# Attention and gated feed-forward on one Trainium2 core: the first unit's attention interleaved over head pairs, and block means placed by a matmul

## The chip, the cores and the metric

The kernel runs on one core of one Trainium2 chip. The metric is the device time of one launch in microseconds (us), the median of several launches. The profile is of one of these launches; its span is 1.7 to 2.1 us shorter than the launch's time. Engines are named as in the profile: PE is TensorE (PEld its weight loads), DVE is VectorE, ACT ScalarE, POOL GpSimd, and SP, which issues DMAs, SyncE. A PE matmul runs at the clock that the throttle grants: full or half (a slow launch also shows 0.95).

## The reference, cut to what matters

The kernel computes attention for 4 batches, 8 heads, 768 tokens, 64 channels, and then a feed-forward layer on all 3072 tokens. A query sees the keys less than 16 positions away, and one summary per block of 32 keys.

```python
k_sum = k.reshape(B, H, nb, block, D).max(axis=3)       # block = 32, nb = 24
v_sum = v.reshape(B, H, nb, block, D).mean(axis=3)
scores_l = scale * q @ k.T, masked to |i - j| < 16
scores_s = scale * q @ k_sum.T + log(block)
a = softmax(concat([scores_l, scores_s]))
x = a @ concat([v, v_sum])                              # per head, then heads side by side
out = x + sigmoid(x @ w_res) * ((gelu(x @ w_gate) * (x @ w_val)) @ w_out)
```

## The kernel before

The work goes in eight units of 384 tokens (half a batch), each with four head pairs. While unit u does its feed-forward, the attention of unit u+1 is woven into its end; at the end of odd units the next batch is prepared too. Only unit 0's attention has nothing to hide behind.

The value tile `vext` holds, for each tile of 64 queries, 96 rows of values (64 plus 16 on each side) and below them 32 rows with the block means, so that one matmul with the masked exponentials P gives both parts and, by a column of ones, the denominator. This product of P with the values is called AV below. The means (`vsum`) are made by a matmul with a constant matrix and then copied, by `vsum_bc`, below every tile. In the code `xn` is the normalised attention output and `xT` its transpose; `sub` counts the three rows of 128 tokens in a unit; MM, AO, TT and SS name PSUM buffers. A column of the feed-forward is 128 of its 1536 hidden channels: four gate and four value matmuls.

```python
def vsum_pair(vs, hp):                     # unit 0: means of one head pair
    for t in range(HT):
        nc.tensor.matmul(vs[96:128, sl], bmat[:, t, :], vext[0][0:BAND, t, ...], start=False, ...)
    nc.vector.tensor_copy(vsum[0][96:128, sl], vs[96:128, sl])
    vsum_bc(0, hp, 0, HT)

def vsum_grp(b, pool, tag):                # other batches: three groups of rows, then moved by DMA
    ...
    nc.vector.tensor_copy(vpart[0:96, :], vs[0:96, :])
    for g, (lo, n) in enumerate(((0, 6), (6, 6), (12, 12))):
        nc.sync.dma_start(out=vsum[b % 2][96 + lo:96 + lo + n, :], in_=vpart[32 * g:32 * g + n, :])

def av_step(u, hp, st, ...):               # 12 matmuls into ao, then the normalisation on DVE
    ...
    nc.vector.reciprocal(rz[:], ao[:, :, :, D:D + 1])
    nc.vector.tensor_mul(xn, ao[:, :, :, 0:D], rz.to_broadcast(...))

# unit 0's attention, after keys, queries and scores
s_step(0, NP - 1, st)
vs = vsum_dense(*TT)
keep_warm(5)                               # matmuls on zeros, result unused
for hp in range(NP):
    vsum_pair(vs, hp)
    av_step(0, hp, st, *(MM if hp % 2 else AO))
    if hp < NP - 1:
        xt_step(0, hp, st, *MM, nc.scalar.copy)      # transpose xn to xT
g0 = half_fo(st, w_gate, 0, 0, KO - 1)               # first feed-forward column
v0 = half_fo(st, w_val, 0, 0, KO - 1)
xt_step(0, NP - 1, st, *TT, nc.scalar.copy)

# end of unit 0: feed-forward of unit 0 and attention of unit 1 (n), woven
s_step(n, 0, nst)
for sub in range(NSUB):
    ffn_step(st, gvT, sub, 0, 4)
    if sub < 2:
        av_step(n, sub, nst); s_step(n, sub + 1, nst)
for sub in range(NSUB):
    ffn_step(st, gvT, sub, 4, 8)
    ...                                              # xt_step 0, av 2, s 3 | xt_step 1, av 3 | xt_step 2
for sub in range(NSUB):
    ffn_step(st, gvT, sub, 8, FO)
    if sub == 1:
        xt_step(n, 3, nst, *TT)
    end_step(u, st, sub)                             # two DVE operations and the store
```

The softmax here doesn't subtract the row's maximum and nothing guards it: scores larger than these inputs give would overflow.

## Time and profile before

The time was 306.99 us (three launches, 305.7 to 307.49). From 115 us to the tail of the last 6 us PE is busy without a gap; what can be won lies before. These are the places:

| place | from, to (us) | PE busy | granted clock |
|---|---|---|---|
| 1, first attention | 16.0, 35.2 | 12.4 of 19.2 | 0.66 |
| 2, end of unit 0 | 54.0, 70.3 | 12.9 of 16.3 | 0.90 |
| 3, end of unit 1 | 91.6, 115.0 | 16.3 of 23.4 | 0.85 |
| the same part of unit 3 | 166.0, 180.0 | 14.0 of 14.0 | 1.00 |

The view of busy time by windows, kernel before. After the window and its length come, for each engine, its busy time and its instructions; then the mean granted clock, the DMA share and GB/s:

```profile
core 0: us, PE busy (x) PEld busy (x) DVE busy (x) ACT busy (x) POOL busy (x), PEclk, DMA share, GB/s
16.00:35.20 19.20, 12.43 (x102) 6.75 (x101) 8.30 (x33) 3.32 (x6) 13.85 (x19) 0.66 1.41 177
53.98:70.30 16.32, 12.93 (x148) 6.58 (x145) 7.84 (x19) 6.95 (x8) 7.96 (x11) 0.90 2.72 152
91.60:115.00 23.40, 16.29 (x159) 7.90 (x159) 11.04 (x24) 7.83 (x9) 6.56 (x9) 0.85 1.35 120
166.00:180.00 14.00, 14.00 (x159) 7.14 (x159) 9.35 (x21) 7.78 (x9) 0.00 (x0) 1.00 0.10 38
```

Place 1. The time line of all engines, kernel before: start, duration, engine, line and operation, output and inputs, number of instructions, and in brackets the idle time before it and what ended it. This is the second head pair:

```profile
22.17 0.81 PE L232 MATMUL vs<-vext,bmat 96*32 96x128 bf16 x6
...
23.02 0.30 DVE L234 CAST vsum<-vs 32x128 bf16<-32x128 f32 x1 [1.18 <-PE vs L232]
23.35 0.36 DVE L256 COPY vext<-vsum 32x768 bf16<-32x768 bf16 x1
23.76 0.54 PE L284 MATMUL ao<-vext,P 128*64 128x65 bf16 x12 [0.78 <-DVE vext L256]
...
24.34 0.20 DVE L288 RECIPROCAL rz<-ao 128x6 f32<-128x6 f32 x1 [0.63 <-PE ao L284]
24.57 0.56 DVE L290 TENSOR_TENSOR xn<-ao,rz 128x384 bf16<-128x384 f32 x1
25.19 0.50 PE L295 MATMUL xp<-ident,xn 128*128 128x128 bf16 x3 [0.88 <-DVE xn L290]
...
34.57 0.48 PE L308 MATMUL g<-xT,w_gate 128*128 128x384 bf16 x1 [0.57 <-ACT xT L297]
```

One engine works at a time: PE, DVE, DVE, PE, DVE, DVE, PE, and only then the next pair. The next pair's means start at 25.62, so a pair takes 3.5 us. The twelve AV matmuls take 0.54 us; later in the same trace they take 0.38: this stretch is at half clock.

Place 3. The chain of waits in order of time (start, us, what), kernel before:

```profile
90.32 0.70 DVE vpart L248
...
92.63 8.21 DMA vsum<-vpart
100.96 1.03 DVE vext L256 x2
```

Three tiny DMAs that only change rows hold the chain for 8.2 us from the issue of the last one. The waits of PE show 7.1 us as the longest wait of AV for P, and P stands behind those broadcasts in the DVE queue.

Place 2. The time line of all engines, kernel before, from the first score of unit 1 to the first gate matmul of unit 1:

```profile
53.98 0.35 PE L266 MATMUL s<-qT,kW 64*128 64x64 bf16 x12
...
54.78 1.28 ACT L270 ACT_TABLE_LOAD   x1
56.08 0.90 ACT L270 ACTIVATE P<-s,bias_t 128x768 bf16<-128x768 f32 x1
...
57.62 0.38 PE L284 MATMUL ao<-vext,P 128*64 128x65 bf16 x12 [2.32 <-DVE P L273]
...
69.94 0.35 DVE L297 COPY xT<-xp 128x384 bf16<-128x384 bf16 x1
...
70.31 0.81 PE L308 MATMUL g<-xT,w_gate 128*128 128x384 bf16 x4
```

PE waits 2.3 us for the first P. The gate's four matmuls are issued by 70.95, when the value matmuls follow: 17.0 us after the first score. I call this the first complete gate.

### The profile page before, as it was taken

The numbers are of one execution on the slowest core, as the hardware profiler recorded it, in microseconds if no ns is written. First come the engines' busy times: TensorE is split into PE (matmuls) and PEld (weight loads), VectorE is DVE, ScalarE is ACT, GpSimd is POOL, SyncE is SP. The second block draws the span as 40 slices with busy tenths as digits, with TensorE's granted clock in tenths as the row PEclk, the third lists the DMA queues.
The fourth block names the chain that finished last, engine by engine and source line by source line (L and its number), as shares of the span: only waits on it lengthen the run. The fifth ranks groups of instructions, "written<-read, shape, count | busy, mean of one in ns | idle before, by whom it ended". The sixth has DMA issues, their size and how long they took to land.

```text
span 305.8 us, 6245 instructions
## 1 busy us (share of the span) xinstructions
PE 274.6 (90%) x2591; PEld 150.4 (49%) x2591; DVE 169.9 (56%) x398; ACT 136.1 (44%) x208; POOL 65.8 (22%) x100
## 2 busy tenths in 40 slices
PE   1674899699994599999999999999999999999993
PEld 1533465345552255645555556555564556456641
DVE  3834562358650665447757674368665854475432
ACT  2811435533653143364656443645556433643310
POOL 8995545357135023003200000000000000000000
PEclk9995699989999599999999999999999999999999
DMA  6999999999999929002900010011000110010001
GB/s 95 167 137 193 200 188 172 202 114 139 238 119 119 193 51 142 2 0 60 122 3 2 36 70 2 1 36 69 2 5 0 52 54 2 0 71 34 2 34 69
DMA packets 58955, 24.45 MB, mean 80 GB/s; under 512 B 37608, under 2 KB 55856, under 8 KB 58928
## 3 DMA queue, kind: packets, MB, share of 16 engines
q0 software_dynamic: 55328, 17.70, 70.8%
q1 hardware_dynamic: 3600, 6.37, 6.0%
q8 instruction: 20, 0.33, 0.5%
q14 instruction: 7, 0.06, 0.1%
HBM read 35.39 MB, written 6.29 MB: 136 GB/s over the span
## 4 chain that ended last, share of the span: by engine, by line
PE 85%; DVE 5%; DMA 4%; ACT 3%; issue 1%; SPq 0%; DVEq 0%; POOLq 0%; ACTq 0%
PE g L308 22%; PE vv L308 20%; PE f L336 20%; PE r L326 7%; PE tp L199 4%; PE ao L284 4%; PE s L266 3%; DMA vsum<-vpart 3%; PE xp L295 2%; DMA k_sb<-in_k_dram 2%; ACT P L270 1%; PE vs L245 1%; DVE vext L256 1%; DVE ks L209 1%; PE vs L232 1%; DVE P L273 1%
## 5 line engine op out<-in xcount | busy, mean ns | idle before, releaser
L315 DVE TENSOR_TENSOR gvT<-ge,vv 128x384 bf16<-128x384 f32 x96 | 52.9, 552 | 51.2 <-PE vv L308 49.7
L308 PE MATMUL g<-xT,w_gate 128*128 128x384 bf16 x384 | 80.8, 330 | 0.6 <-ACT xT L297 0.6
L314 ACT ACTIVATE ge<-g 128x384 f32<-128x384 f32 x96 | 47.0, 490 | 73.2 <-DVE gvT L315 44.5
L308 PE MATMUL vv<-xT,w_val 128*128 128x384 bf16 x384 | 79.0, 328 | 0.0
L336 PE MATMUL f<-w_out,gvT 128*128 128x512 bf16 x288 | 70.9, 388 | 0.0
L308 PEld LDWEIGHTS <-w_val 128*128 128x128 bf16 x384 | 37.7, 98 | 26.5 <-issue 2.1
L94 POOL DMA_DIRECT2D vext<-in_v_dram x43 | 32.6, 762 | 73.5 <-PE ao L284 41.3
L308 PEld LDWEIGHTS <-w_gate 128*128 128x128 bf16 x384 | 35.5, 98 | 24.8 <-issue 3.2
L270 ACT ACTIVATE P<-s,bias_t 128x768 bf16<-128x768 f32 x32 | 28.8, 900 | 41.4 <-PE s L266 40.9
L336 PEld LDWEIGHTS <-gvT 128*128 128x128 bf16 x288 | 27.4, 100 | 31.6 <-issue 2.7
L273 DVE TENSOR_TENSOR P<-P,maskt 128x768 bf16<-128x768 bf16 x32 | 17.7, 554 | 20.7 <-ACT P L270 20.5
L284 PE MATMUL ao<-vext,P 128*64 128x65 bf16 x384 | 13.2, 208 | 14.1 <-DVE P L273 10.5
L326 PE MATMUL r<-w_res,xT 128*128 128x512 bf16 x96 | 25.6, 391 | 0.0
L284 PEld LDWEIGHTS <-P 128*64 128x64 bf16 x384 | 9.7, 118 | 26.7 <-DVE P L273 16.8
L209 DVE TENSOR_REDUCE ks<-kW 128x24 bf16<-128x768 bf16 x16 | 15.2, 953 | 12.1 <-ACT kW L206 12.1
L341 DVE SCALAR_TENSOR_TENSOR th<-th,f 128x512 f32<-128x512 f32 x24 | 16.3, 679 | 7.5 <-PE f L336 7.5
L329 ACT ACTIVATE th<-r 128x512 f32<-128x512 f32 x24 | 14.3, 595 | 10.4 <-PE r L326 10.1
L206 ACT COPY kW<-tp 128x768 bf16<-128x768 bf16 x16 | 12.8, 797 | 13.0 <-PE tp L199 13.0
L290 DVE TENSOR_TENSOR xn<-ao,rz 128x384 bf16<-128x384 f32 x32 | 17.8, 557 | 1.1
L343 DVE SCALAR_TENSOR_TENSOR o<-th,xn 128x512 f32<-128x512 f32 x24 | 16.6, 692 | 0.8
L219 ACT COPY qT<-tp 128x768 bf16<-128x768 bf16 (+1 forms) x20 | 13.4, 671 | 8.0 <-PE tp L199 8.0
L199 PE MATMUL tp<-ident,k_sb 96*64 96x96 bf16 x256 | 9.8, 227 | 6.5 <-DMA k_sb<-in_k_dram 6.5
(64 smaller groups left out, 187.8 us busy)
## 6 DMA issues: line engine op xcount, KB each, us to landing
out_dram<-o SPq DMA_DIRECT2D x24, 256.0 KB, 2.0
vext<-in_v_dram POOLq DMA_DIRECT2D x35, 96.0 KB, 8.3
k_sb<-in_k_dram POOLq DMA_DIRECT2D x3, 768.0 KB, 12.5
q_sb<-in_q_dram POOLq DMA_DIRECT2D x3, 768.0 KB, 15.4
v_sb<-in_v_dram POOLq DMA_DIRECT2D x4, 384.0 KB, 15.1
w_gate<-in_moe_w_gate_dram POOLq DMA_DIRECT2D x6, 256.0 KB, 8.3
w_val<-in_moe_w_val_dram POOLq DMA_DIRECT2D x6, 256.0 KB, 8.8
w_out<-in_moe_w_out_dram POOLq DMA_DIRECT2D x3, 512.0 KB, 14.3
```

The lines of the kernel that those rows point to most:

```text
L94: nc.gpsimd.dma_start(out=vext[b % 2][r0:r0 + hi - lo, t, :, 0:D], in_=v[b, :, lo:hi, :].rearrange("h p d -> p h d"))
L199: nc.tensor.transpose(tp[hh * 64:hh * 64 + 64, j, :], src[:, 2 * hp + hh, j, :], ident[0:PP, 0:PP])
L209: nc.vector.tensor_reduce(out=ks.rearrange("d (t n) -> d t n", n=2), in_=kw[:, :, OWN:OWN + QT].rearrange("d t (n w) -> d t n w", w=BLK), ...
L270: nc.scalar.activation(P.rearrange("p a t q -> p a (t q)"), s[:, :, 0:TU], AF.Exp, scale=scale, bias=bias_t[:])
L273: nc.vector.tensor_mul(Pf, Pf, maskt.unsqueeze(1).to_broadcast([128, 2 * HT, QT]))
L284: nc.tensor.matmul(ao[64 * e:64 * e + 64, sub, hh, :], P[:, hh, t, :], vext[b % 2][:, half * HT + t, 2 * hp + hh, :], start=True, stop=Tru ...
L290: nc.vector.tensor_mul(xn, ao[:, :, :, 0:D], rz.to_broadcast([128, NSUB, 2, D]))
L308: nc.tensor.matmul(acc[:, 0:TU], w[:, ko, fs], st["xT"][:, ko, :], start=(ko == 0), stop=(ko == KO - 1))
L314: nc.scalar.activation(ge[:], g[:, 0:TU], AF.Gelu)
L315: nc.vector.tensor_mul(gvT[:, fo, :], ge[:], vv[:, 0:TU])
L326: nc.tensor.matmul(r[:], st["xT"][:, ko, ss], w_res[:, ko, :], start=(ko == 0), stop=(ko == KO - 1))
L336: nc.tensor.matmul(st["f", sub][:], gvT[:, fo, ss], w_out[:, fo, :], start=(fo == 0), stop=(fo == FO - 1))
```

## The change

Place 1 is to run as a pipeline over head pairs: the means' copies move to ACT, the block part of AV becomes a second matmul that reads `vsum` directly, and warm matmuls stand between the pairs. Place 3 is to lose its DMA: a matmul with a 0/1 matrix `place` moves the rows. In place 2 the AV of unit 1 goes behind most of the feed-forward. The diff, cut to its core:

```diff
+        for g in range(3):
+            select(place[32 * g:32 * g + 32, :], ALU.not_equal, 1.0, 6 * g, -1, 1)
 ...  vsum_pair
-            nc.vector.tensor_copy(vsum[0][96:128, sl], vs[96:128, sl])
-            vsum_bc(0, hp, 0, HT)
+            nc.scalar.copy(vsum[0][96:128, 2 * hp:2 * hp + 2, 0:D],
+                           vs[96:128, sl].rearrange("p (h d) -> p h d", d=D))
 ...  vsum_grp
-            nc.vector.tensor_copy(vpart[0:96, :], vs[0:96, :])
-            for g, (lo, n) in enumerate(((0, 6), (6, 6), (12, 12))):
-                nc.sync.dma_start(out=vsum[b % 2][96 + lo:96 + lo + n, :], in_=vpart[32 * g:32 * g + n, :])
+            nc.scalar.copy(vpart[0:96, :], vs[0:96, :])
+
+        def vsum_place(b, pool, tag):
+            vs = pool.tile([128, DM], F32, tag=tag, name="vs")
+            nc.tensor.matmul(vs[96:128, :], place[:], vpart[0:96, :], start=True, stop=True)
+            nc.scalar.copy(vsum[b % 2][96:128, :, 0:D], vs[96:128, :].rearrange("p (h d) -> p h d", d=D))
 ...  unit 0's attention
+        vs = vsum_dense(*TT)
         s_step(0, NP - 1, st)
-        vs = vsum_dense(*TT)
-        keep_warm(5)
+        vsum_pair(vs, 0)
+        vsum_pair(vs, 1)
+        keep_warm(3)
         for hp in range(NP):
-            vsum_pair(vs, hp)
-            av_step(0, hp, st, *(MM if hp % 2 else AO))
-            if hp < NP - 1:
-                xt_step(0, hp, st, *MM, nc.scalar.copy)
+            if hp >= 2:
+                vsum_pair(vs, hp)
+            av_part(0, hp, st, *(MM if hp % 2 else AO), blocks=False)   # rows 0 to 95, from vext
+            av_part(0, hp, st, blocks=True)                             # rows 96 to 127, from vsum
+            av_norm(hp, st)
+            if hp:
+                xt_step(0, hp - 1, st, *(MM if hp % 2 else SS), nc.scalar.copy)
+            if 0 < hp < NP - 1:
+                keep_warm(2)
 ...  odd units: the means by vsum_grp at column 10 (unit 1) or 8, vsum_place one column later,
 ...  unit 1 takes all keys before all queries, broadcasts in pairs at columns 10 and 11
 ...  end of unit 0
                 for sub in range(NSUB):
                     ffn_step(st, gvT, sub, 0, 4)
-                    if sub < 2:
-                        av_step(n, sub, nst)
-                        s_step(n, sub + 1, nst)
+                    s_step(n, sub + 1, nst)
                 for sub in range(NSUB):
                     ffn_step(st, gvT, sub, 4, 8)
-                    ...
+                for hp in range(NP):
+                    av_step(n, hp, nst, *(MM if hp % 2 else AO))
+                    if hp:
+                        xt_step(n, hp - 1, nst, *TT)
+                        ffn_step(st, gvT, hp - 1, 8, FO)
+                        end_step(u, st, hp - 1)
+                xt_step(n, 3, nst, *TT)
```

More of the change, by code (lines that the diff above doesn't have):

```diff
@@ L72 @@
     vext = [const.tile([128, NT, H, D + 1], BF16, name=f"vext{i}") for i in range(2)]
-    vsum = [const.tile([128, DM], BF16, name=f"vsum{i}") for i in range(2)]
+    vsum = [const.tile([128, H, D + 1], BF16, name=f"vsum{i}") for i in range(2)]
+    place = const.tile([PP, 32], BF16, name="place")
     vpart = const.tile([128, DM], BF16, name="vpart")
@@ L141 @@
         nc.vector.memset(bden[:, 12:24], 1.0 / BLK)
+        nc.vector.memset(place[:], 0.0)
+        nc.vector.memset(vsum[0][96:128, :, D:D + 1], 1.0)
         vext_consts(0)
@@ L247, in vsum_grp @@
                                      skip_group_check=True)
-            nc.vector.tensor_copy(vpart[0:96, :], vs[0:96, :])
-            for g, (lo, n) in enumerate(((0, 6), (6, 6), (12, 12))):
-                nc.sync.dma_start(out=vsum[b % 2][96 + lo:96 + lo + n, :],
-                                  in_=vpart[32 * g:32 * g + n, :])
+            nc.scalar.copy(vpart[0:96, :], vs[0:96, :])
[3 more added lines that the diff above has]
+            nc.scalar.copy(vsum[b % 2][96:128, :, 0:D], vs[96:128, :].rearrange("p (h d) -> p h d", d=D))
         def vsum_bc(b, hp, lo, hi):
-            src = vsum[b % 2][96:128, hp * 128:hp * 128 + 128].rearrange("p (h d) -> p h d", d=D)
+            src = vsum[b % 2][96:128, 2 * hp:2 * hp + 2, 0:D]
             src = src.unsqueeze(1).to_broadcast([32, hi - lo, 2, D])
@@ L274, in s_step, with av_part @@
             st["P", hp] = P
-        def av_step(u, hp, st, pool=ps_o, tag="ao"):
+        def av_part(u, hp, st, pool=ps_o, tag="ao", blocks=None):
             b, half = u // 2, u % 2
             P = st["P", hp]
-            ao = pool.tile([128, NSUB, 2, D + 1], F32, tag=tag, name="ao")
+            rows = slice(0, 128) if blocks is None else slice(96, 128) if blocks else slice(0, BAND)
+            if not blocks:
+                st["ao", hp] = pool.tile([128, NSUB, 2, D + 1], F32, tag=tag, name="ao")
+            ao = st["ao", hp]
             for sub in range(NSUB):
@@ L283, in av_step, with av_norm @@
                         t = 2 * sub + e
-                        nc.tensor.matmul(ao[64 * e:64 * e + 64, sub, hh, :], P[:, hh, t, :],
-                                         vext[b % 2][:, half * HT + t, 2 * hp + hh, :],
-                                         start=True, stop=True, skip_group_check=True)
+                        rhs = vsum[0][rows, 2 * hp + hh, :] if blocks else \
+                            vext[b % 2][rows, half * HT + t, 2 * hp + hh, :]
+                        nc.tensor.matmul(ao[64 * e:64 * e + 64, sub, hh, :], P[rows, hh, t, :], rhs,
+                                         start=blocks is None or (not blocks and sub == 0 and hh == 0),
+                                         stop=blocks is not False,
+                                         skip_group_check=True)
+        def av_norm(hp, st):
+            ao = st["ao", hp]
             rz = work.tile([128, NSUB, 2, 1], F32, tag="rz", name="rz")
@@ L290, in av_step @@
             nc.vector.tensor_mul(xn, ao[:, :, :, 0:D], rz.to_broadcast([128, NSUB, 2, D]))
+        def av_step(u, hp, st, pool=ps_o, tag="ao"):
+            av_part(u, hp, st, pool, tag)
+            av_norm(hp, st)
         def xt_step(u, ko, st, pool, tag, copy=nc.vector.tensor_copy):
@@ L358 @@
                 s_step(0, hp - 1, st)
+        vs = vsum_dense(*TT)
         s_step(0, NP - 1, st)
-        vs = vsum_dense(*TT)
-        keep_warm(5)
+        vsum_pair(vs, 0)
+        vsum_pair(vs, 1)
+        keep_warm(3)
         for hp in range(NP):
-            vsum_pair(vs, hp)
-            av_step(0, hp, st, *(MM if hp % 2 else AO))
-            if hp < NP - 1:
-                xt_step(0, hp, st, *MM, nc.scalar.copy)
+            if hp >= 2:
+                vsum_pair(vs, hp)
+            av_part(0, hp, st, *(MM if hp % 2 else AO), blocks=False)
+            av_part(0, hp, st, blocks=True)
+            av_norm(hp, st)
+            if hp:
+                xt_step(0, hp - 1, st, *(MM if hp % 2 else SS), nc.scalar.copy)
+            if 0 < hp < NP - 1:
+                keep_warm(2)
         g0 = half_fo(st, w_gate, 0, 0, KO - 1)
         v0 = half_fo(st, w_val, 0, 0, KO - 1)
-        xt_step(0, NP - 1, st, *TT, nc.scalar.copy)
+        xt_step(0, NP - 1, st, *SS, nc.scalar.copy)
         vext_consts(1)
         vext_edges(1)
-        nc.vector.memset(vsum[1][96:128, :], 0.0)
         kw_consts(1)
@@ L396 @@
                         home = TT if i % 2 else AO
-                        if i % 2:
-                            q_step(q_sb[nb], nb, 0, S, i // 2, *home)
-                        else:
-                            k_step(nb, i // 2, *home)
-                    if fo == (10 if u == 1 else 4):
-                        vsum_grp(nb, *SS)
-                    if u > 1 and fo >= 8:
-                        vsum_bc(nb, fo - 8, 0, NT)
+                        if u == 1:
+                            kq, hp = divmod(i, NP)
+                        else:
+                            hp, kq = divmod(i, 2)
+                        if kq:
+                            q_step(q_sb[nb], nb, 0, S, hp, *home)
+                        else:
+                            k_step(nb, hp, *home)
+                    if fo == (10 if u == 1 else 8):
+                        vsum_grp(nb, *SS)
+                    if fo == (11 if u == 1 else 9):
+                        vsum_place(nb, *SS)
+                    if u > 1 and fo >= 10:
+                        vsum_bc(nb, 2 * (fo - 10), 0, NT)
+                        vsum_bc(nb, 2 * (fo - 10) + 1, 0, NT)
             nst = new_unit() if n < NU else None
@@ L413 @@
                     ffn_step(st, gvT, sub, 0, 4)
-                    if sub < 2:
-                        av_step(n, sub, nst)
-                        s_step(n, sub + 1, nst)
+                    s_step(n, sub + 1, nst)
                 for sub in range(NSUB):
                     ffn_step(st, gvT, sub, 4, 8)
-                    if sub == 0:
-                        xt_step(n, 0, nst, *TT)
-                        av_step(n, 2, nst)
-                        s_step(n, 3, nst)
-                    elif sub == 1:
-                        xt_step(n, 1, nst, *TT)
-                        av_step(n, 3, nst)
-                    else:
-                        xt_step(n, 2, nst, *TT)
-                for sub in range(NSUB):
-                    ffn_step(st, gvT, sub, 8, FO)
-                    if sub == 1:
-                        xt_step(n, 3, nst, *TT)
-                    end_step(u, st, sub)
+                for hp in range(NP):
[5 more added lines that the diff above has]
+                xt_step(n, 3, nst, *TT)
                 st = nst
```

## The prediction

> **What bounds it now.** TensorE: the chain of waits is 85% PE; by the table of windows PE is busy without a gap from 115 us on. The loss lies before, in three places of the time line.
> 1. First attention, 16 to 35.2 us: PE busy 12.4 of 19.2 us at clock 0.66. Four head pairs run in series, about 3.5 us each: block means on PE (0.5 to 0.8), copy on DVE (0.30), broadcast into the value tile on DVE (0.36 to 0.68), AV, reciprocal and scale on DVE (0.79), transpose. The last gate matmul of the first column is at 34.57.
> 2. End of unit 0, 54.0 to 70.3: PE waits 2.3 us for the first masked P, behind a 1.28 us table load and a 0.90 us exp; 3.4 us at half clock follow.
> 3. End of unit 1, 91.6 to 115.0: the means go to their rows by DMA, 8.2 us in the chain; PE waits 7.1 us for P behind it on DVE, then 6.8 us at half clock. Unit 3, where this is hidden, takes 13.9 us there, unit 1 takes 23.4.
>
> **What the change does.**
> - Place 1: copies of the means move to ACT, the broadcast leaves the chain (12 short matmuls a pair instead, 0.35 us), pairs overlap, warm matmuls fill. Summing traced durations in the new order puts the last gate matmul at about 27.4 and, at full clock, the third column at 29.2 instead of 37.0: 7.8 us gained. Every weight chunk lands (issue plus time to landing) about 2 us or more before its new use, with 0.8 us of delay by three selects.
> - Place 3: a matmul (0.22 us) and an ACT copy (0.6) replace the DMA. The first score waits 0.8 us for the PSUM buffer; residual and feed-forward hide the rest. About 15 us instead of 23.4: 8.3 gained.
> - Place 2 gets worse. AV moves behind the feed-forward, probably since value tiles land as late as 54.2 us and this stage now starts at about 46. Scores still wait 1.9 us for table load and exp through the single score buffer. Then norms (0.79), xT copies (0.36) and end steps (1.41) share the DVE queue: 4x0.79+4x0.36+3x1.41 = 8.8 us, the last xT copy behind the last end step, where before it came ahead of two. First complete gate of unit 1 about 18.4 us after the first score, against 17.0: 1.4 lost. PE gaps (0.9, 1.4, 0.9 us) may halve the clock: the Trainium skill, "TensorE: Matmul & The Clock Gate", Part 1, has a free-running activity window of about 3.4 us, and this trace agrees (half-clock stretches of 3.4, 6.8 and 13.7 us). About 1 more, on average.
> - Units 3 and 5: +0.2 us each for the place matmul, at most some tenths for broadcasts packed in pairs.
>
> **Sum.** 307.0 - 7.8 - 8.3 + 2.4 + 0.6 = 293.9; I say 293.8 us, 8 in 10 between 290.5 and 298.0. Faster by over 2%: 0.95; within 2%: 0.04; slower: 0.01.
>
> **Signs.** Right if unit 0's third column starts near 29 us at full clock; unit 1's AV no longer waits 7.1 us for P and its end takes about 15 us; the end of unit 0 takes 17 us or more, PE waiting for xT behind DVE's end steps.
> **Wrong if** the clock stays half in the first attention (+3), value heads or tiles land late, the end of unit 0 gains after all (-2), or ACT, with new copies, holds back the gelu.

## The result, and the profile after

The changed kernel takes 298.37 us (median, 296.95 to 298.43), against 306.36 us for the kernel before over the same launches (305.7 to 307.49). The ratio is 0.9725, 95% interval 0.9687 to 0.9763. Ratios here are the mean time of one kernel's fast launches over that of the other's in the same rounds, so not quite the ratio of the medians quoted. It is 8.0 us faster; the prediction said 13.2 less than 306.99, and 298.4 lies 0.4 us above its range of 290.5 to 298.0.

The two profiled spans differ by more, 305.8 - 294.9 = 10.9 us. The profile after is the luckiest of its launches (296.95 us, mean clock 0.999); the other four took 298.1 to 298.4 with a mean clock of 0.992 to 0.994. A clock of 0.993 over some 265 us of record is about 3.7 us at half clock, so about one window of 3.4 us, and costs 1.45 us (298.4 - 296.95). The profile before came from a launch of 307.5, the longest of its four. Stage by stage, from these two profiles:

| stage | before | after | change | predicted |
|---|---|---|---|---|
| start to third feed-forward column of unit 0 | 36.8 | 32.84 | -4.0 | -7.8 |
| first score to first complete gate of unit 1 | 17.0 | 17.7 | +0.7 | +1.4, +1 more for clock |
| end of unit 1's columns to unit 2's first gate | 23.2 | 14.9 | -8.3 | -8.3 |
| units 3 and 5, together | | | +1.1 | +0.6 |

Place 1. The time line of PE alone, kernel after (the columns are as before):

```profile
17.66 0.80 PE L237 MATMUL vs<-vext,bmat 96*32 96x128 bf16 x6 [0.53 <-ACT vsum L239]
18.80 1.06 PE L370 MATMUL wp<-warm 128*128 128x512 bf16 x2 [0.33 <-issue]
19.79 0.54 PE L296 MATMUL ao<-vext,P 96*64 96x65 bf16 x12
20.26 0.54 PE L296 MATMUL ao<-vsum,P 32*64 32x65 bf16 x12
...
31.04 0.47 PE L328 MATMUL g<-xT,w_gate 128*128 128x384 bf16 x1 [0.57 <-ACT xT L317]
...
32.84 0.81 PE L328 MATMUL g<-xT,w_gate 128*128 128x384 bf16 x4
```

The waits of PE for DVE are gone, and the pairs follow each other closely. But the AV matmuls still take 0.54 us, so half clock. The first record of full clock in this trace is at 31.4 us. (The windows view of the kernel after prints a clock of 1.00 for this stretch:

```profile
14.00:32.84 18.84, 17.19 (x175) 10.00 (x172) 6.76 (x30) 6.72 (x14) 14.20 (x22) 1.00 1.36 156
```

There is no clock record before 31.4, and the view shows 1.00 where there is none. The durations of the matmuls tell the truth.) PE is busy 17.2 of 18.8 us: the place went from waiting to PE-bound at half clock.

Place 3. The time line of all engines, kernel after:

```profile
88.33 0.39 PE L257 MATMUL vs<-vpart,place 96*32 96x512 bf16 x1
...
88.76 0.58 ACT L258 CAST vsum<-vs 32x512 bf16<-32x512 f32 x1 [0.48 <-PE vs L257]
...
89.39 0.35 PE L273 MATMUL s<-qT,kW 64*128 64x64 bf16 x12 [0.67 <-ACT vsum L258]
...
93.23 0.38 PE L296 MATMUL ao<-vext,P 128*64 128x65 bf16 x12
...
103.23 1.03 PE L328 MATMUL g<-xT,w_gate 128*128 128x384 bf16 x4
```

From the place matmul to the means at their rows it is 1.0 us, where the DMA took 8.2. PE waits 0.67 us for the score buffer that the means borrow, and AV comes with no wait.

Place 2. The time line of all engines, kernel after:

```profile
50.00 0.35 PE L273 MATMUL s<-qT,kW 64*128 64x64 bf16 x12
...
53.05 0.35 PE L273 MATMUL s<-qT,kW 64*128 64x64 bf16 x12 [1.94 <-ACT P L277]
...
65.93 0.33 PE L315 MATMUL xp<-ident,xn 128*128 128x128 bf16 x3 [1.09 <-DVE xT L317]
...
66.50 0.69 DVE L363 SCALAR_TENSOR_TENSOR o<-th,xn 128x512 f32<-128x512 f32 x1
67.11 0.35 DVE L317 COPY xT<-xp 128x384 bf16<-128x384 bf16 x1
67.52 0.32 PE L328 MATMUL g<-xT,w_gate 128*128 128x384 bf16 x1 [0.77 <-DVE xT L317]
```

The score waits 1.94 us for ACT, as foretold, and the last xT copy stands behind the last end step on DVE while PE waits for it.

### The profile page after: what moved, and what is told of

Same layout as the page of the kernel before. It is cut to its first block, busy times and chain, and to the rows that moved or that the text cites. A ratio compares the mean times of both kernels' runs of the same rounds, so it can differ in the third digit from the quotient of the medians.

```text
span 294.9 us, 6313 instructions
## 1 busy us (share of the span) xinstructions
PE 273.0 (93%) x2619; PEld 151.0 (51%) x2644; DVE 164.4 (56%) x388; ACT 140.4 (48%) x218; POOL 66.8 (23%) x103
## 4 chain that ended last, share of the span: by engine, by line
PE 89%; DVE 4%; ACT 3%; DMA 2%; issue 1%; POOLq 0%; DVEq 0%; ACTq 0%
PE g L328 23%; PE vv L328 21%; PE f L356 20%; PE r L346 7%; PE tp L204 4%; PE ao L296 4%; PE s L273 3%; PE xp L315 2%; DMA k_sb<-in_k_dram 2%; PE vs L250 1%; DVE o L363 1%; ACT P L277 1%; DVE th L361 1%; PE wp L370 1%; PE vs L237 1%
## 5 line engine op out<-in xcount | busy, mean ns | idle before, releaser
L356 PE MATMUL f<-w_out,gvT 128*128 128x512 bf16 x273 | 65.7, 379 | 1.4 <-issue 0.9
L328 PEld LDWEIGHTS <-w_val 128*128 128x128 bf16 x384 | 37.6, 98 | 27.5 <-issue 3.4
L277 ACT ACTIVATE P<-s,bias_t 128x768 bf16<-128x768 f32 x32 | 28.8, 901 | 29.0 <-PE s L273 28.4
L280 DVE TENSOR_TENSOR P<-P,maskt 128x768 bf16<-128x768 bf16 x32 | 17.7, 554 | 21.2 <-ACT P L277 21.2
L346 PE MATMUL r<-w_res,xT 128*128 128x512 bf16 x88 | 24.2, 381 | 0.5 <-issue 0.2
L349 ACT ACTIVATE th<-r 128x512 f32<-128x512 f32 x24 | 14.3, 595 | 9.6 <-PE r L346 9.2
L304 DVE RECIPROCAL rz<-ao 128x6 f32<-128x6 f32 x32 | 6.1, 192 | 20.3 <-PE ao L296 20.3
L296 PEld LDWEIGHTS <-P 128*64 128x64 bf16 (+2 forms) x432 | 10.7, 119 | 13.0 <-DVE P L280 5.1
```

The lines of the kernel that those rows point to most:

```text
L277: nc.scalar.activation(P.rearrange("p a t q -> p a (t q)"), s[:, :, 0:TU], AF.Exp, scale=scale, bias=bias_t[:])
L296: nc.tensor.matmul(ao[64 * e:64 * e + 64, sub, hh, :], P[rows, hh, t, :], rhs, start=blocks is None or (not blocks and sub == 0 and hh == ...
L328: nc.tensor.matmul(acc[:, 0:TU], w[:, ko, fs], st["xT"][:, ko, :], start=(ko == 0), stop=(ko == KO - 1))
L346: nc.tensor.matmul(r[:], st["xT"][:, ko, ss], w_res[:, ko, :], start=(ko == 0), stop=(ko == KO - 1))
L356: nc.tensor.matmul(st["f", sub][:], gvT[:, fo, ss], w_out[:, fo, :], start=(fo == 0), stop=(fo == FO - 1))
```

## The experiments

Each edit is against the kernel after. All twelve kernels gave correct results. "Before" was timed beside them each time, at 306.5 to 307.1 us. The kernel after was not: differences to it go across sessions, and the experiments ran on four chips.

### One part at a time: a_only, c_only, a_and_c

`a_only` keeps only place 1 of the change, `c_only` only place 3, `a_and_c` both, with the old order at the end of unit 0. The edit of `a_and_c`; the others also put back the other part's old lines:

```diff
                     ffn_step(st, gvT, sub, 0, 4)
-                    s_step(n, sub + 1, nst)
+                    if sub < 2:
+                        av_step(n, sub, nst)
+                        s_step(n, sub + 1, nst)
                     ...  (the old order of the kernel before)
```

> Only the first attention is changed (the old end of unit 0, the old DMA for the means). If the three places add, this gains what the first score of unit 1 gained in the two profiles, 53.98 to 50.00, so about 4.0 us: 302.4. Rival: without the late AV the gain cannot be kept, since AV of unit 1 now comes at about 53.6 us, before the last value tiles (54.7 us): then PE waits about 1 us more there and the time is about 303.4. Clock: the first attention runs at half clock until after its end, as in the profile of the changed kernel.

> Only the means of units 2, 4 and 6 go to their rows by a matmul (with the key-first order and the packed broadcasts). The two profiles give 8.3 us gained at the end of unit 1 and 0.55 us lost in each of units 3 and 5: about 299.2 us, the first 90 us as before. Rival: part of the 8.3 us came with the other changes (other clock windows); then it is over 300.5.

> The changed kernel with the old order at the end of unit 0. My theory: the late AV costs as much as it saves. The old order waits for the value tiles (last landing about 54.7 us, AV wanted at 53.6), so from the first score to the first complete gate about 18 us against 17.7 with the late order: 298 to 299 us, same as the changed kernel. Rival 1: late AV is needed, the old order waits several us for values, over 300. Rival 2: late AV is a pure loss, under 297.5.

Measured: `a_only` 304.58 us (ratio 0.9934, interval 0.989 to 0.9978), 2.2 us less than before. `c_only` 298.98 us (ratio 0.9782, interval 0.9726 to 0.9838), 7.8 less; one of its four launches took 302.19, with the half clock of the first attention reaching to 38.3. `a_and_c` 296.97 us (ratio 0.97, interval 0.9662 to 0.9738), 9.8 less. So places 1 and 3 add: 2.2 + 7.8 = 10.0. Place 3 is most of the change, and place 1 brings about half of what two single profiles let one expect (4.0). Both forecasts for `a_only` (302.4, rival 303.4) were missed. In its profile, the fastest of its launches, the first score does come at 50.0, and PE then waits 0.6 us for value tiles, the rival's cause; where the rest goes in the other launches stays open.

For the late AV, `a_and_c` is 1.4 us faster than the kernel after by the medians. The two ratios' intervals overlap, and the two were timed in different sessions. From the first score to the first complete gate `a_and_c` took 17.1 us, with a half-clock window from 54.7 to 58.1 inside, the kernel after 17.7 in the launch that had no such window. `warm_full` (below) has the late order too, and such a window inside, from 53.8 to 57.2: it took 19.0. So the late AV brought nothing, and probably costs one to two microseconds: 1.4 by the medians, 1.9 in this stage by one pair of launches with a window each. The forecast (298 to 299, no difference) was missed; the time is that of rival 2, a pure loss. The time line of PE in `a_and_c` shows what it was for:

```profile
53.66 0.34 PE L296 MATMUL ao<-vext,P 128*64 128x65 bf16 x9 [2.54 <-DVE P L280]
54.78 0.27 PE L296 MATMUL ao<-vext,P 128*64 128x65 bf16 x3 [0.78 <-DMA vext<-in_v_dram]
```

The old order, now 4 us earlier, runs into the last value tiles and waits 0.78 us for their DMA.

### The DVE queue at the end of unit 0: late_act and hybrid

`late_act` only moves the four xT copies of this stage from DVE to ACT:

```diff
-                        xt_step(n, hp - 1, nst, *TT)
+                        xt_step(n, hp - 1, nst, *TT, nc.scalar.copy)
 ...
-                xt_step(n, 3, nst, *TT)
+                xt_step(n, 3, nst, *TT, nc.scalar.copy)
```

> The changed kernel with the xT copies at the end of unit 0 on ACT. If the DVE queue (norms, xT copies, end steps) sets the end of unit 0, four copies of 0.35 us leave it and the last one no longer stands behind an end step: first score to first complete gate 16.7 instead of 17.7, time about 1 us less (297.4). Rival: PE's own order or the AV sets it, no change (298.4).

Measured: 295.75 us (ratio 0.9651, interval 0.9623 to 0.968), so 2.6 us less than the kernel after. The stage took 16.5 us instead of 17.7. The time line of all engines in `late_act`:

```profile
65.61 1.05 PE L328 MATMUL g<-xT,w_gate 128*128 128x384 bf16 x4
65.81 0.48 ACT L317 COPY xT<-xp 128x384 bf16<-128x384 bf16 x1 [1.54 <-PE xp L315]
66.01 0.69 DVE L363 SCALAR_TENSOR_TENSOR o<-th,xn 128x512 f32<-128x512 f32 x1
```

The copy now runs beside the end step on DVE instead of behind it. The gate's last matmul waits only some 0.2 us for it (four gate matmuls take 0.65 us without a wait; the value matmuls follow here after 0.89). The DVE theory stands: 1.2 us foretold as 1.0. The other 1.4 us fits the clock: three of four launches have a mean clock of 1.0 and the fourth 0.996, where four of five launches of the kernel after had 0.992 to 0.994. The same step without the warm matmuls repeats it: three of four launches of `no_warm` have 0.992 to 0.994, all four of `no_warm_act` 0.996 to 1.0. With shorter gaps on PE the half-clock window mostly stayed away. That the gaps decide it was not varied by itself.

`hybrid` keeps the scores early and puts AV ahead of the second third of the feed-forward, with the xT copies on DVE:

```diff
-                for sub in range(NSUB):
-                    ffn_step(st, gvT, sub, 4, 8)
                 for hp in range(NP):
-                    av_step(n, hp, nst, *(MM if hp % 2 else AO))
-                    if hp:
-                        xt_step(n, hp - 1, nst, *TT)
-                        ffn_step(st, gvT, hp - 1, 8, FO)
-                        end_step(u, st, hp - 1)
-                xt_step(n, 3, nst, *TT)
+                    av_step(n, hp, nst)
+                    if hp < NSUB:
+                        ffn_step(st, gvT, hp, 4, 8)
+                        xt_step(n, hp, nst, *TT)
+                for sub in range(NSUB):
+                    ffn_step(st, gvT, sub, 8, FO)
+                    if sub == 0:
+                        xt_step(n, 3, nst, *TT)
+                    end_step(u, st, sub)
```

> The changed kernel with another order at the end of unit 0: scores still early, AV of pair hp straight after the last score, ahead of feed-forward columns 4 to 8, so that norms and xT copies are out of the DVE queue before the end steps. If the order in the DVE queue is what the late AV loses, first score to first complete gate takes about 14.5 us instead of 17.7 and the time is about 295. The value tiles land (54.8 us) just before AV 0 (55.9). Rival: PE wait for ACT at the start (1.9 us) and clock dominate: under 1 us gained.

Measured: 295.24 us median; the fast launches took 294.96 to 295.42 (ratio 0.9608, interval 0.9558 to 0.9657). Its profile fell in a slow launch (303.17 us, clock 0.949), so its stages are not compared. About 3 us less than the kernel after, as foretold. Part of it is again the clock (0.996 to 1.0 in the fast launches); the rest, without a profile of a fast launch, can't be split further.

### The warm matmuls: no_warm, warm_full, warm_narrow, warm_short, warm_rows

`no_warm` takes the seven warm matmuls of the first attention out:

```diff
-        keep_warm(3)
 ...
-            if 0 < hp < NP - 1:
-                keep_warm(2)
```

> The changed kernel without its seven warm matmuls in the first attention. In the profile they take 3.0 us of PE at half clock while PE has hardly a gap, and the clock rises only at 31.4, after the gate and value matmuls began. My theory: they buy nothing there, so the last gate matmul of column 0 comes at about 28.8 instead of 31.04 and the time falls by 1 to 2.5 us. Rival: they are what lets the clock rise at 31.4; without them it rises a window (3.4 us) later or the chain's latency takes their place: no gain, or a loss of up to 1.5 us.

Measured: 295.28 us (ratio 0.9614, interval 0.9565 to 0.9663), 3.1 us less than the kernel after, more than the 1 to 2.5 expected. The time line of PE in `no_warm`:

```profile
27.96 0.48 PE L328 MATMUL g<-xT,w_gate 128*128 128x384 bf16 x1 [0.57 <-ACT xT L317]
...
30.00 0.81 PE L328 MATMUL g<-xT,w_gate 128*128 128x384 bf16 x4
```

The last gate matmul of column 0 comes 3.1 us earlier (31.04 before), which is the seven warm matmuls at half clock, about 0.43 us each. The clock still rises once the gate and value matmuls run, here at 28.8. So the fillers bought nothing: they did not fill gaps of PE, PE had hardly any.

The other four ask what it would take. They use 8, 6 and 6 warm matmuls instead of 3, 2 and 2, in four shapes:

```diff
-                nc.tensor.matmul(wp[:], warm[:, 0:128], warm[:], ...)          # warm_full keeps this
+                nc.tensor.matmul(wp[0:32, :], warm[:, 0:32], warm[:], ...)     # warm_narrow: 32 columns
+                for c in range(8):                                             # warm_short: 8 x 64 long
+                    nc.tensor.matmul(wp[:, c * 64:c * 64 + 64], warm[:, 0:128], warm[:, c * 64:c * 64 + 64], ...)
+                nc.tensor.matmul(wp[:], warm[0:32, 0:128], warm[0:32, :], ...) # warm_rows: 32 rows
```

> The changed kernel with 8, 6 and 6 warm matmuls (128x128 weights, 512 columns) for 3, 2 and 2. Theory 'array work': the clock rises when a 3.4 us window holds about 1.2 us or more of full-array matmuls, whatever the share of busy time; then it rises within about 22 to 25 us here, and the attention runs at full clock. Rival 'busy time or luck of the window': PE was 90 to 100% busy from 17.7 to 28 us in the changed kernel without a rise, so more warm matmuls change nothing and the rise stays near 31.

> As warm_full, but each warm matmul has 32 weight columns instead of 128: same time on PE, a quarter of the array. Theory 'array work': no early rise, the clock stays half until the gate and value matmuls, so the first gate comes late (about 36 us and later). Rival 'busy time': the same rise as in warm_full.

> As warm_full, but each warm matmul of 512 columns is cut into eight of 64 columns, same weights. warm_full and warm_narrow both raised the clock at 21 to 23 us, so it is not the share of the array. Theory 'stream length': short matmuls, as those of scores, AV and transposes, count less than long ones; then no rise before the gate and value matmuls begin. Rival: any filler raises it at 21 to 23 us.

> As warm_full, but each warm matmul contracts over 32 rows instead of 128: same time on PE, same 512 columns. Weight width and stream length did not matter for the rise of the clock (21 to 23 us in all three fillers). Theory 'rows': what counts is the rows of the array that moving data uses; the attention's own matmuls use 32, 64 or 96 rows in most of their time and do not raise it. Then no rise here before the gate and value matmuls (over 28 us). Rival: any 3 us of dense filler raises it, at 21 to 24 us.

| kernel | time (launches) | first record of full clock | last gate matmul of column 0 |
|---|---|---|---|
| after | 298.37 (4) | 31.4 | 31.04 |
| no_warm | 295.28 (4) | 28.8 | 27.96 |
| warm_full | 298.6 (2) | 23.1 | 31.73 |
| warm_narrow | 296.4 (2) | 21.1 | 30.25 |
| warm_short | 299.57 (1) | 20.6, half again 27.5 to 30.9 | 33.73 |
| warm_rows | 303.57 (1) | 39.1 | 36.82 |

`warm_full` got the clock: the time line of PE shows its third set of fillers at full clock,

```profile
26.72 1.46 PE L370 MATMUL wp<-warm 128*128 128x512 bf16 x6
...
31.73 0.32 PE L328 MATMUL g<-xT,w_gate 128*128 128x384 bf16 x1 [0.57 <-ACT xT L317]
```

and yet its first gate is 0.7 us later than in the kernel after and 3.8 us later than in `no_warm`. What the full clock gives here, the fillers that raise it eat.

`warm_narrow` refutes my theory of array work: with a quarter of the columns the clock rose as early. `warm_short` refutes stream length: pieces of 64 raised it too (it fell again in a window with a PE gap of 1.23 us). `warm_rows` is the one that did not raise it, though PE was busy all the time. The time line of PE and, in the second fence, the windows view of `warm_rows`:

```profile
18.43 3.59 PE L370 MATMUL wp<-warm 32*128 32x512 bf16 x8
21.95 0.54 PE L296 MATMUL ao<-vext,P 96*64 96x65 bf16 x12
...
33.72 1.25 PE L328 MATMUL g<-xT,w_gate 128*128 128x384 bf16 x3
```

```profile
18.40:33.70 15.30, 15.30 (x138) 7.49 (x138) 2.42 (x7) 1.74 (x5) 9.97 (x14) 1.00 1.38 182
```

Busy 15.3 of 15.3 us, and half clock throughout (0.54 us for twelve AV matmuls; 1.00 stands again for "no record"). So of the four things varied (busy time, weight columns, stream length, rows), the rows of the array that the moving data fill is the one on which the rise depended in these launches. `warm_rows` is a single launch, but `no_warm` says the same: in the 3.4 us before its rise, 25.4 to 28.8, PE was busy only 2.84 us, all of it in matmuls and transposes of 128 rows; in the 3.4 us before that, 22.0 to 25.4, it was busy all the time, 2.1 us of it in matmuls of 32 and 96 rows, and the clock stayed half. This fits the change: its second AV matmul fills 32 rows, the first one 96, scores 64. How rows are weighed, and where the threshold lies, stays open; these runs don't give it.

### Together: no_warm_act and best

`no_warm_act` is `no_warm` with `late_act`. `best` is `no_warm` with a third order at the end of unit 0:

```diff
                 s_step(n, 0, nst)
                 for sub in range(NSUB):
                     ffn_step(st, gvT, sub, 0, 4)
+                for sub in range(NSUB):
                     s_step(n, sub + 1, nst)
-                for sub in range(NSUB):
                     ffn_step(st, gvT, sub, 4, 8)
                 for hp in range(NP):
-                    av_step(n, hp, nst, *(MM if hp % 2 else AO))
-                    if hp:
-                        xt_step(n, hp - 1, nst, *TT)
-                        ffn_step(st, gvT, hp - 1, 8, FO)
-                        end_step(u, st, hp - 1)
-                xt_step(n, 3, nst, *TT)
+                    av_step(n, hp, nst)
+                    if hp < NSUB:
+                        ffn_step(st, gvT, hp, 8, FO)
+                    xt_step(n, hp, nst, *TT, nc.scalar.copy)
+                for sub in range(NSUB):
+                    end_step(u, st, sub)
```

> no_warm and late_act together. If the two are independent: 298.4 - 3.1 - 2.6 = 292.7 us, first score to first complete gate 16.5. Rival: late_act's gain over the changed kernel was partly a missed half-clock window (its own profile shows only 1.2 us less in that stage), so together they give only 4.3: 294.1.

> The changed kernel without warm matmuls and with a third order at the end of unit 0: the first third of feed-forward for all three rows of tokens covers the table load, scores go between the second thirds, AV pairs between the last thirds, xT copies on ACT, end steps last. From no_warm: first score at 47.2. If the gains of the parts add: AV 0 waits about 0.8 us for the value tiles (54.8), first score to first complete gate 14.5 instead of 17.7, so 295.3 - 3.2 = 292.1 us. Rival: the value tiles come later than that or the half clock falls into it: 293.5 or more.

Measured: `no_warm_act` 292.53 us (ratio 0.9534, interval 0.9507 to 0.956), which is the sum of the two gains: 298.37 - 3.09 - 2.62 = 292.66. `best` 291.31 us (290.69 to 291.94, ratio 0.9492, interval 0.9458 to 0.9525), against 307.09 for the kernel before beside it. The time line of all engines in `best`:

```profile
47.51 0.35 PE L273 MATMUL s<-qT,kW 64*128 64x64 bf16 x12
47.79 2.76 PE L356 MATMUL f<-w_out,gvT 128*128 128x512 bf16 x12
...
60.75 0.34 PE L315 MATMUL xp<-ident,xn 128*128 128x128 bf16 x3 [0.95 <-DVE xn L306]
60.93 1.05 PE L328 MATMUL g<-xT,w_gate 128*128 128x384 bf16 x4
```

Twelve feed-forward matmuls cover the table load and the first exp, the last xT copy waits for no end step, and the first complete gate comes 14.3 us after the first score. One wait of 0.95 us is left in this stage. The 0.8 us wait for value tiles that the forecast (292.1) counted did not come.

## Why the prediction was right or wrong

- **Place 3, right.** A matmul and an ACT copy for the DMA: "about 15 us instead of 23.4"; measured 14.9 against 23.2. The 0.8 us wait for the PSUM buffer was 0.67. `c_only` confirms it: 7.8 us gained in the medians, where 8.3 less the 1.1 lost in units 3 and 5 gives 7.2.
- **Place 1, the mechanism right, the size wrong.** The step that failed is "pairs overlap, warm matmuls fill", and with it "at full clock, the third column at 29.2". The copies and broadcasts did leave the chain. But the warm matmuls filled nothing: PE had hardly any gaps left (busy 17.2 of 18.8 us), and seven fillers took 3.1 us of it (`no_warm`). Nor did they keep the clock, which rose at 31.4. The third column came at 32.84, so the term of -7.8 us measured -4.0. Without them the third column starts at 30.00, still after an attention at half clock: 0.8 us from the 29.2 predicted. The prediction named the half clock as a risk of 3 us; that the column came about 3.6 us late fits this size by luck, since taking the fillers out gives 2.8 of it back. With more fillers the clock did rise (`warm_full`), and the stage became no shorter. What full clock without fillers would give, no run shows. A smaller part is the second pair's means waiting 0.53 us for the first pair's copy on ACT.
- **Place 2, right in kind.** The late AV gains nothing; 17.7 us against 17.0 in the profile (predicted 18.4), because the DVE queue sets the end (`late_act`: 1.2 us less when four copies leave it). The stated reason for moving AV, the late value tiles, is there (`a_and_c`), but it is 0.78 us. The half-clock window, put at "about 1 more, on average", costs 1.45 us in four of five launches. The profile after is the one launch without it; `warm_full`, with the same order, has it inside this stage, which takes 19.0 us there: 2.0 more than before, where 2.4 was predicted.
- **Units 3 and 5, mis-sized.** Predicted +0.6 together, measured +1.1. A place matmul takes 0.32 us out of the stream of PE (151.91 to 152.23), not 0.22. The rest, about 0.23 us each, was not taken apart.
- **The sum.** The terms are off by 3.8 us in place 1 and 0.5 in units 3 and 5, and place 2 was about as predicted. The gain was 8.0 us against 13.2. About 1 us of the difference is left open; one possible reason is that the profile before, on which all terms stood, was of the longest of the launches timed with it, with clock windows that the others didn't all have.

## What to carry to other kernels

Before adding matmuls that only keep the clock up, look whether PE has gaps for them; without gaps they cost their full time, twice as much at half clock, and here taking them out was worth 3.1 us. When work is moved to an engine's queue late in a stage, ask what the next stage needs first from that queue, and put that ahead of the rest or on another engine. Three tiny DMAs that only change rows took 8.2 us here; a matmul with a 0/1 matrix and a copy did it in 1.0.

## What the Trainium skill lacked or had wrong

- "TensorE: Matmul & The Clock Gate", Part 1, says of the warm-up that "whatever you issue in your first ~3.4 µs runs at 1.2 GHz; everything after runs at 2.4 GHz". Not so here: in `warm_rows` PE was busy 15.3 of 15.3 us from 18.4 on and stayed at half clock until 39.1. In these launches the rise went with the number of rows that the matmuls fill (first full clock at 39.1 with 32-row fillers, one launch; at 20.6 to 23.1 with 128-row fillers), and the page doesn't say that rows count.
- The same page, "Why this matters for your kernels", asks for no PE gaps over about 3 us to keep the clock. That row alone was not enough here: the kernel before fell to half clock at 22.2 after a window (18.8 to 22.2) in which PE was busy 1.7 of 3.4 us and no gap was longer than 0.9 us.
- The same page, Part 4, says that transposes don't count as PE-busy in the same way. This agrees in kind with the first attention in `no_warm`, which up to its first gate matmul consists of transposes and matmuls of 32, 64 and 96 rows and did not raise the clock (PE busy 8.4 of 9.0 us from 15.9 to 24.9); no run here separates the transposes.
- No page read for this case says that a profile's clock column may show 1.00 where there is no clock record. Here it did for all of the half-clock time before the first record (31.4 us in the kernel after); the duration of a repeated matmul shape (0.54 against 0.38 us) tells it.
